# Part of V goes to the lower 64 partitions of two slots, in transfers of eight rows

## The chip, the cores and the metric

The kernel runs on one core of one Trainium2 chip. The metric is the device time of one execution in microseconds, as the median of several runs. A profile of one execution is read beside it: it lists each instruction of the engines (PE for matmuls, PEld for its weight loads, DVE, ACT, POOL, and SP, which issues the loads), and each packet of the 16 DMA engines.

## What is computed

Two layers of a decoder, each a cached attention with grouped heads and then a small network, for eight sequences and one new token each. Cut to the part that matters here, the attention:

```python
def _A_ref(x, k_cache, v_cache, wq, wo):          # x: (8, 1, 448)
    q = (x @ wq).reshape(B, 1, 16, 256).transpose(0, 2, 1, 3)
    k = jnp.repeat(k_cache, 2, axis=1)            # k_cache, v_cache: (8, 8, 4096, 256), bf16
    v = jnp.repeat(v_cache, 2, axis=1)
    scores = jnp.einsum("bhqd,bhkd->bhqk", q, k) * 256 ** -0.5
    p = softmax(scores)
    o = jnp.einsum("bhqk,bhkd->bhqd", p, v)
    return o.transpose(0, 2, 1, 3).reshape(B, 1, 4096) @ wo
x = x + _A_ref(_layernorm(x), k_cache, v_cache, wq, wo)
x = x + _B_ref(_layernorm(x), w1, w2, w3, w4)
...
```

Both layers use the same two caches. Each cache has 8 sequences x 8 heads x 4096 rows x 256 numbers of two bytes: 2 MB for each head of each sequence, 134 MB for a cache.

## The kernel before

**Tiles.** A head of K or V is read as 128 partitions of 32 consecutive rows each, 16 KB in a partition. It is cut into four pieces (`NCH`), each 4 KB of every partition: 512 KB. A piece lives in one of 31 slots of SBUF (`slots`, `NSLOT`). A load brings one, two or four neighbouring pieces at once into neighbouring slots (512 KB, 1 MB or 2 MB); `chunks` (lines 444 to 460) makes these groups, and its argument `most` is the largest. The planner may split a group when it finds no run of free slots.

**Pairs of heads.** Work goes by layer, sequence `b` and pair of heads `m`. `kpart` (line 836) takes the eight K pieces of a pair: most are transposed by DVE (line 914, into another slot), some by PE and ACT (lines 832 and 892), then PE makes the scores (lines 902, 923, 951) into the PSUM bank `psS`. Softmax follows (lines 983 to 1030); the probabilities are transposed into a small tile `pT`. `vpart` (line 1034) takes the eight V pieces of the pair. In the form used here PE multiplies each piece by its probabilities with four matmuls of 128 partitions x 512 columns (line 1089) into the bank `psV`. `pN` is a pair of small tiles that holds probabilities in another order for the pieces whose K was not transposed by DVE.

**Order.** The second layer of sequence b needs the first layer of the same sequence, so the body from line 1226 on goes through the sequences: `turn(b)` ends layer 0 of b and begins layer 1, then come the pairs of layer 1 of b and of layer 0 of b+1. `weave` lays the loads of K and V one between the other into one list, and SP issues all loads of the kernel in that order on one queue. `schedule` (line 168) is a planner that runs while the kernel is built: it simulates the engines with a cost for each operation, chooses a slot for each piece, and so fixes the order of instructions on every engine. In it an issue takes SP 330 ns (line 292), and a load starts 3.3 us after its issue at the earliest and moves at 410 or 415 bytes per ns (line 294).

**Waits.** A load waits on SP for the instructions that read its slot last. What uses a piece waits for the semaphore of its slot, which a load raises by 16 when it has landed, a sixteenth of that for each of the DMA engines that take part (line 1264).

Of the kernel before, what the change touches and what calls it, by code (L numbers as in the profile page):

```python
# [3 lines left out]
P = 128  # L4
B = 8
# [6 lines left out]
NCH = 4  # L12
NSLOT = 31
SMALL = 218
SLOT = 2048
# [5 lines left out]
NN = ((1, 0, 1, 1), (0, 0, 1, 1))  # L21
NZ = 2
WIDE = ((1, 0),)
MOST = (4, 4, 4, 2)
DRY4 = 4000.0
STILL = (False, False)
# [46 lines left out]
class Unit:  # L73


    def __init__(self, name, emit, nbytes, slotted=True):
        self.name, self.emit, self.nbytes, self.slotted = name, emit, nbytes, slotted
        self.wide = None
        self.slot = self.sem = self.val = None
        self.op = None  # L80
        self.readers = []
        self.land = None
        self.evs = [None, None]
        self.raw, self.source = False, None
        self.group, self.lead, self.pair = [self], None, None


class Plan:
# [79 lines left out]
    def schedule(self, order, nslot):  # L168
# [8 lines left out]
        free = {e: 0.0 for e in ("pe", "dve", "act", "pool", "sp")}  # L177
# [68 lines left out]
        while remaining or nxt[0] < len(order):  # L246
# [8 lines left out]
            while nxt[0] < len(order):  # L255
                u = order[nxt[0]]
                if any(d.end is None for d in u.op.deps):
                    break
                start = max(free["sp"], max((d.end + 80 for d in u.op.deps), default=0.0))
                us = u.group  # L260
                if u.slotted:
                    if len(us) == 1:
                        best = single(t)
                    else:
                        best, short = run(t, len(us))
                        if short and len(us) == 4 and transfer < t + DRY4:
                            order.insert(nxt[0] + 1, self.split(u, users))
                            us = u.group
                            best, short = run(t, len(us))
                        one = single(t)  # L270
                        if (len(us) == 2 and short and transfer < t + DRY and one is not None and slot_free[one][0] <= t + 1e-6
                                and len(slot_free) > bool(raw or u.raw) + sum(1 for o in ready["act"] if o.target is not None)
                                and free["sp"] <= t + 1e-6):
                            order.insert(nxt[0] + 1, self.split(u, users))
                            us, best = u.group, one
                    held = sum(1 for x in {o.target for o in ready["act"] if o.target is not None} if x.slot is None)
                    if best is None or len(slot_free) < len(us) + bool(raw or u.raw) + held:
                        break
                    start = max([start] + [slot_free[best + k][0] for k in range(len(us))])
                if start > t + 1e-6:  # L280
                    sp_next = start
                    break
                if u.slotted:
                    for k, x in enumerate(us):
                        _, waits = slot_free.pop(best + k)
                        x.slot = best + k
                        for w in waits:
                            u.op.deps[w] = True
                        live.append(x)
                        if x.raw:  # L290
                            raw.add(x)
                free["sp"] = start + 330.0
                if u.emit is not None:
                    transfer = max(start + 3300.0, transfer) + (P * 4096 * len(us) / 415.0 if len(us) > 1 else u.nbytes / 410.0)
                    land = transfer + 2000.0
                else:
                    land = start
                for x in us:
                    x.land = land
                u.op.on = "sp"  # L300
                seq["sp"].append(u.op)
                done(u.op, land, 0.0)
                nxt[0] += 1
                progress = True
            for e in ("pe", "dve", "act", "pool"):
# [15 lines left out]
                o = min(cand, key=lambda o: (o.prio, o.name))  # L321
# [37 lines left out]
def bass_interleave_layers__gqa_block_cached__mixer_s_mlp__decode_kernel(  # L359
# [26 lines left out]
    slots = [slab[:, SLOT * i:SLOT * i + SLOT] for i in range(NSLOT)]  # L386
# [6 lines left out]
    ident = sb("ident", [P, P], bf)  # L393
# [3 lines left out]
    pT = [sb(f"pT{i}", [P, 192], bf) for i in range(NP)]  # L397

    pN = [sb(f"pN{i}", [P, 48], bf) for i in range(NZ)]
# [17 lines left out]
    psS = [nc.alloc_psum_tensor(f"psS{i}", [P, 512], f32) for i in range(NS)]  # L417
    psV = [nc.alloc_psum_tensor(f"psV{i}", [P, 512], f32) for i in range(NV)]
# [7 lines left out]
    plan = Plan()  # L426
# [14 lines left out]
    U_wo = [rows(f"wo{i}", wo_sb[:, 8 * i:8 * i + 8, :], wo_src[:, 8 * i:8 * i + 8, :], P * 7168 * 1.1) for i in range(4)]  # L441
    U_w4 = [rows("w4", w4_sb[:, :, :], B_w4.rearrange("(t m) n -> m t n", m=P), P * 12544 * 1.1)]

    def chunks(cache, b, h, name, skip=(), most=2):


        src = cache[b, h].rearrange("(p j) d -> p (j d)", p=P)

        def emit(e, u):
            c, n = int(u.name[-1]), len(u.group)  # L450
            return e.dma_start(slab[:, SLOT * u.slot:SLOT * (u.slot + n)], src[:, SLOT * c:SLOT * (c + n)])
        us = [None if c in skip else Unit(f"{name}{c}", emit, P * 4096) for c in range(NCH)]
        for i in range(0, NCH, most):
            group = [u for u in us[i:i + most] if u is not None]
            if len(group) == most:
                plan.load(group[0], mates=group[1:])
            else:
                for u in group:
                    plan.load(u)
        return us  # L460


    Bc = Buf()
# [350 lines left out]
    def apart(t):  # L814

        return t.rearrange("p (a c u r) -> p a c r u", a=4, u=3, r=4)[:, :, :, :, 0:3:2]
# [19 lines left out]
    def kpart(at, layer, b, m, kept, most=2):  # L836
# [12 lines left out]
        nS[0] += 1  # L849
        p.x = x  # L850
        p.y = y = free_p.pop(0)
        p.z = z = free_n.pop(0) if layer == 0 and m > 1 else None
        plan.prio = at
        p.K, p.kload = [], []
        for s in range(2):
# [169 lines left out]
        for c in range(nn if z is None else 0):  # L1025
            ss = slice(sum(c >= w for w in nns), 2)
            add("act", lambda e, c=c, ss=ss: e.activation(apart(pT[y])[:, :, c, :, ss], xs.rearrange("p (a c r s) -> p a c r s", a=4, c=4, r=4)[:, :, c, :, ss],
                                                          ACT.Exp, scale=INV_SQRT_DH), 230, [], [BpT[y]], [bS[x]], prio=pr, name=n + f"pn{c}")
        add("pool", lambda g: g.partition_all_reduce(db, rs, P, ReduceOp.add), 450, [B_["pm"]], [B_["gm"]], prio=pr + 1, name=n + "db")
        R = add("dve", lambda e: e.reciprocal(rc, db), 70, [B_["gm"]], [Brc[y]], prio=pr + 1, name=n + "rc")  # L1030
        R.deps = {d: data or d.eng == "dve" for d, data in R.deps.items()}
# [2 lines left out]
    def vpart(at, p, still, bank, most, aside):  # L1034
# [2 lines left out]
        own_ = lambda s, c: z is not None and c < p.nns[s]  # L1037
        Bp = lambda s, c: [BpN[z]] if own_(s, c) else [BpT[y], BpZ[y]]
        plan.prio = at
        p.V = [u for s in range(2) for u in chunks(A_v_cache, b, 2 * m + s, f"{n}V{s}", (), most)]  # L1040
        p.vload = [u for u in p.V if u.lead is None]
        if layer == 0:
            out_, bo = o1[b % 2][:, 8 * m:8 * m + 8], Bo1[b % 2][m]
        else:
# [28 lines left out]
        else:  # L1073
# [3 lines left out]
            for s in range(2):  # L1077
                for c in range(NCH):
                    u = p.V[NCH * s + c]

                    def pv(e, u=u, c=c, s=s):
                        for i in range(4):
                            o = 12 * (NCH * i + p.place(s, c)) + 4 * s
                            w = pN[z][:, 12 * i + 4 * s:12 * i + 4 * s + 8] if own_(s, c) else pT[y][:, o:o + 8]
                            if c < p.nns[s]:
                                v = slots[u.slot][:, 512 * i:512 * i + 512].rearrange("p (k d) -> p k d", k=2)
                            else:
                                v = slots[u.slot].rearrange("p (k j d) -> p j k d", k=2, j=4)[:, i]
                            last = e.matmul(psV[x][32 * i:32 * i + 8, :].rearrange("p (k d) -> p k d", k=2), w, v,  # L1089
                                            start=(s == 0 and c == 0), stop=(s == 1 and c == NCH - 1))  # L1090
                        return last
                    o = add("pe", pv, 430, Bp(s, c), [], [bV[x]], [u], prio=at + 0.02 * (NCH * s + c), name=f"{n}V{s}{c}", n=4)
                    if s or c:
                        o.deps[first] = True
                    else:
                        first = o
# [24 lines left out]
                for d in Bq1[b].readers + Bq1[b].writers:  # L1121
                    O.deps.setdefault(d, False)
        free_p.append(y)
        if z is not None:
            free_n.append(z)

    Bst = [{k: Buf() for k in ("pm", "gm", "mx")} for _ in range(NS)]
    red, Bred = sf[:, 0:8], [Bs[k] for k in ("sq", "f", "f1")]
# [129 lines left out]
    for o in seq["sp"]:  # L1258
        u = o.unit
        if u.emit is None:  # L1260
            u.sem = None
            continue
        if u.slotted:
            slot_n[u.slot] += 16
            u.sem, u.val = slot_sem[u.slot], slot_n[u.slot]
        else:
            u.sem, u.val = nc.alloc_semaphore(f"s_{u.name}"), 16
# [124 lines left out]
```

## Time and profile before

| | |
|---|---|
| median of 3 runs | 1097.92 us (1097.88 to 1098.41) |
| the profiled execution | 1098.74 us |
| its span, first to last instruction | 1095.7 us |
| mean clock granted to TensorE | 0.619 of full speed |
| busy: DVE, PE, ACT, POOL | 832.6, 756.3, 207.8, 71.4 us |
| read from HBM | 446.77 MB, 408 GB/s over the span |
| loads of V: 2 MB, 1 MB, 512 KB | 50, 149, 14 |
| loads of K: 2 MB, 1 MB, 512 KB | 44, 71, 2 |

Times in the views count from the first instruction. A row of windows gives, for a stretch of time, the busy time of each engine with its number of instructions, the granted clock of TensorE, the share of time in which the 16 DMA engines were busy (it may pass 1 where packets of two queues overlap on one engine) and the rate in GB/s. A row of DMA issues gives the tile, the issuing queue, the count, the size of one and the median time from issue to landing. A row of waits says who waited for whom, how long in all, how often, and the longest.

### The profile page before, as it was taken

What the parts mean: (1) busy time and instruction counts of PE and PEld (TensorE: products, weight loads), DVE (VectorE), ACT (ScalarE), POOL (GpSimd) and SP (SyncE); (2) the same over time, 40 slices, a digit from 0 to 9 for tenths busy, and PEclk for the clock granted to TensorE, in tenths of its full rate; (3) what the DMA queues carried; (4) which work ended last, traced back from release to release, by engine and by line L of the source; (5) the groups of instructions that cost most, each with busy time, mean ns of one, the idle gap of its engine ahead of it and who ended that gap; (6) DMA issues with size and microseconds to landing.
All of it is one profiled execution on the core that took longest, in us unless ns stands there. A gap on an engine that the chain in (4) does not pass through costs nothing.

```text
span 1095.7 us, 33703 instructions
## 1 busy us (share of the span) xinstructions
PE 756.3 (69%) x15400; PEld 526.6 (48%) x15400; DVE 832.6 (76%) x1595; ACT 207.8 (19%) x314; POOL 71.4 (7%) x232
## 2 busy tenths in 40 slices
PE   2566586778577865867767787577666786676864
PEld 2355454465346543555436554355444654356533
DVE  4999459964997499955899469984799739995572
ACT  1032121112021211203112032121221121121210
POOL 0000000000000000000000000000100000000000
PEclk9997566556655665556655556555655566555665
DMA  9999999999999999999999999999999999999994
GB/s 353 406 419 420 395 406 426 422 412 408 429 423 415 412 425 427 421 405 409 424 426 420 411 412 429 426 417 394 427 427 423 419 399 428 427 422 411 410 427 176
DMA packets 54846, 448.94 MB, mean 410 GB/s; under 512 B 5536, under 2 KB 11568, under 8 KB 14128
## 3 DMA queue, kind: packets, MB, share of 16 engines
q1 hardware_dynamic: 54704, 446.80, 98.4%
q8 instruction: 120, 1.97, 0.7%
q14 instruction: 22, 0.18, 0.0%
HBM read 446.77 MB, written 0.01 MB: 408 GB/s over the span
## 4 chain that ended last, share of the span: by engine, by line
DVE 39%; DMA 24%; PE 21%; issue 9%; ACT 3%; POOL 0%; POOLq 0%; DVEq 0%
DVE slots L914 29%; DMA slots<-in_A_k_cache_dram 16%; DMA slots<-in_A_v_cache_dram 8%; PE psV L1089 6%; PE psS L923 5%; DVE pT L1021 2%; PE psT L678 2%; ACT slots L892 2%; PE psS L902 2%; DVE slots L1102 1%; PE psV L1063 1%; PE psT L607 1%; PE psK L832 1%; PE psT L1138 1%; DVE qe L643 1%
## 5 line engine op out<-in xcount | busy, mean ns | idle before, releaser
L914 DVE STREAM_TRANSPOSE slots<-slots 128x1024 bf16<-128x1024 bf16 x544 | 649.4, 1228 | 33.0 <-DMA slots<-in_A_k_cache_dram 24.3
L923 PE MATMUL psS<-qe,slots 128*128 128x8 bf16 x5760 | 225.3, 175 | 152.6 <-DVE slots L914 111.5
L923 PEld LDWEIGHTS psS<-qe,slots 128*128 128x128 bf16 x5760 | 191.1, 104 | 238.5 <-DVE slots L914 176.0
L1089 PE MATMUL psV<-slots,pT 128*8 128x512 bf16 x1528 | 181.1, 550 | 17.5 <-DMA slots<-in_A_v_cache_dram 9.5
L892 ACT COPY slots<-psK 128x1024 bf16<-128x1024 bf16 x80 | 78.8, 1014 | 168.0 <-PE psK L832 167.6
L832 PE MATMUL psK<-ident,slots 128*128 128x128 bf16 x640 | 74.2, 301 | 4.2 <-DMA slots<-in_A_k_cache_dram 4.1
L1100 ACT ACTIVATE slots<-psV 128x512 bf16<-128x512 f32 x48 | 29.0, 605 | 218.5 <-PE psV L1089 218.4
L985 POOL PARTITION_ALL_REDUCE small<-small x64 | 23.8, 372 | 693.5 <-DVE small L983 582.4
L832 PEld LDWEIGHTS psK<-ident,slots 128*128 128x128 bf16 x640 | 61.1, 138 | 7.0 <-DMA slots<-in_A_k_cache_dram 4.9
L1063 PE MATMUL psV<-pT,slots 128*128 128x2 bf16 x1568 | 50.9, 166 | 17.1 <-DMA slots<-in_A_v_cache_dram 15.9
L951 PE MATMUL psS<-slots,qe 128*8 128x512 bf16 x184 | 55.4, 587 | 6.7 <-DVE slots L914 5.4
L1063 PEld LDWEIGHTS psV<-pT,slots 128*128 128x128 bf16 x1568 | 47.3, 104 | 19.7 <-DMA slots<-in_A_v_cache_dram 16.1
L1089 PEld LDWEIGHTS psV<-slots,pT 128*8 128x8 bf16 x1528 | 31.5, 90 | 50.5 <-issue 20.9
L1021 DVE STREAM_TRANSPOSE pT<-psS 128x128 bf16<-128x128 bf16 x64 | 44.9, 702 | 6.5 <-PE psS L1013 4.7
L1006 ACT ACTIVATE pT<-psS 128x128 bf16<-128x128 f32 x56 | 15.5, 277 | 178.7 <-DVE psS L1003 178.6
L1066 DVE TENSOR_REDUCE small<-psV 128x8 f32<-128x32 f32 x16 | 2.8, 174 | 58.5 <-PE psV L1063 58.5
L1111 PE MATMUL psV<-same,slots 128*128 128x4 bf16 x320 | 14.0, 166 | 43.0 <-DVE slots L1102 36.9
L630 DVE TENSOR_TENSOR qe<-psT,small 128x32 bf16<-128x32 f32 x32 | 6.1, 190 | 48.2 <-PE psS L923 34.3
L902 PE MATMUL psS<-qo,slots 128*128 128x2 bf16 x768 | 27.8, 167 | 17.6 <-ACT slots L892 10.5
L1102 DVE TENSOR_TENSOR slots<-psV,slots 128x512 bf16<-128x512 f32 x48 | 32.3, 672 | 10.0 <-ACT slots L1100 10.0
L902 PEld LDWEIGHTS psS<-qo,slots 128*128 128x128 bf16 x768 | 24.0, 101 | 25.4 <-ACT slots L892 17.1
L1111 PEld LDWEIGHTS psV<-same,slots 128*128 128x128 bf16 x320 | 11.8, 102 | 49.2 <-issue 40.8
(170 smaller groups left out, 805.8 us busy)
## 6 DMA issues: line engine op xcount, KB each, us to landing
slots<-in_A_v_cache_dram SPq DMA_DIRECT2D x149, 1024.0 KB, 9.7
slots<-in_A_v_cache_dram SPq DMA_DIRECT2D x50, 2048.0 KB, 19.1
slots<-in_A_k_cache_dram SPq DMA_DIRECT2D x44, 2048.0 KB, 18.1
slots<-in_A_k_cache_dram SPq DMA_DIRECT2D x71, 1024.0 KB, 13.7
slots<-in_A_v_cache_dram SPq DMA_DIRECT2D x14, 512.0 KB, 8.1
wo_sb<-in_A_wo_dram SPq DMA_DIRECT2D x4, 896.0 KB, 19.5
wq_sb<-in_A_wq_dram SPq DMA_DIRECT2D x3, 1024.0 KB, 9.1
w_sb<-in_B_w_dram SPq DMA_DIRECT2D x1, 1568.0 KB, 16.9
```

Of the source, the lines that this page charges most:

```text
L832: last = e.transpose(tile[:, j * P:(j + 1) * P], slots[u.slot][:, o:o + P], ident[:, :])
L892: return e.copy(slots[u.slot][:, 1024 * t:1024 * t + 1024], tile)
L902: last = e.matmul(o, slots[u.slot][:, i:i + P], q, start=(cc == 0), stop=(cc == 1))
L914: return e.transpose(o, i)
L923: last = e.matmul(o, slots[u.slot][:, i:i + P], qe[:, 128 * k + 64 * s + 8 * g:128 * k + 64 * s + 8 * g + 8], start=(g == 0), stop=(g == 7))
L951: last = e.matmul(o, q, K[:, lo:hi + 1:hi - lo, :, g, :], start=(g == 0), stop=(g == 7))
L1021: add("dve", lambda e: e.transpose(pZ[:, :, 0:3:2].rearrange("p n s r -> p n r s"), psS[x][:, 128:192].bitcast(bf).rearrange("p (n r s) -> ...
L1063: last = e.matmul(o, slots[u.slot][:, i:i + P], w, start=(j == 0), stop=(j == 7))
L1089: last = e.matmul(psV[x][32 * i:32 * i + 8, :].rearrange("p (k d) -> p k d", k=2), w, v, start=(s == 0 and c == 0), stop=(s == 1 and c == ...
L1100: add("act", lambda e: e.activation(part(0), psV[x][:, :], ACT.Copy), 590, [], [Bhalf[0]], [bV[x]], [v], prio=at - 1, name=n + "ve0").targ ...
L1102: add("dve", lambda e: e.tensor_tensor(part(1), psV[x][:, :], part(0), ALU.subtract), 590, [Bhalf[0]], [Bhalf[1]], [bV[x]], [v], prio=at - ...
L1111: last = e.matmul(to[:, 4 * cc:4 * cc + 4].rearrange("p (s h) -> p s h", s=2), part(k // 2)[:, i:i + P], w, start=(k == 0), stop=(k == 3))
```

## The change

`LOW(layer, b, m, s)` picks one head in eight places: the first head of pair 0, for layer 0 of sequence 0 and for layer 1 of sequences 0 to 6. Of this head's V the last of the four pieces (`LOWC` = 3) is loaded in another way. Before, its 512 KB went, as part of a larger load, to 128 partitions of one slot. Now the rows of partitions 0 to 63 go to the lower 64 partitions of one slot, and the rows of partitions 64 to 127 to the lower 64 partitions of a second slot. Each half is moved by eight transfers of eight rows of 4 KB, the rows of one transfer being eight partitions apart; all eight raise the slot's semaphore, by 128 together. The head's other pieces are loaded as 1 MB and 512 KB. The two halves are separate units in the list of loads, so a load of K stands between them.

PE multiplies such a piece with eight matmuls of 64 partitions instead of four of 128: for the second half the probabilities of partitions 64 to 127 are needed on partitions 0 to 63. One matmul with the identity moves them into free columns of `psS`, and ACT copies them into a tile of `pN`. The product waits for both halves and for this tile. In the planner an issue of such a half costs eight times 330 ns, and its 256 KB are priced at 410 bytes per ns. The diff, without its empty lines:

```diff
@@ -21,6 +21,10 @@
 NN = ((1, 0, 1, 1), (0, 0, 1, 1))
 NZ = 2
 WIDE = ((1, 0),)
+LOWS, LOWC = 0, 3
+def LOW(layer, b, m, s):
+    return s == LOWS and m == 0 and (layer == 1 and b < B - 1 or layer == 0 and b == 0)
 MOST = (4, 4, 4, 2)
 DRY4 = 4000.0
 STILL = (False, False)
@@ -83,6 +87,8 @@
         self.evs = [None, None]
         self.raw, self.source = False, None
         self.group, self.lead, self.pair = [self], None, None
+        self.upper = None
+        self.issues = 1
 class Plan:
@@ -289,7 +295,7 @@
                         live.append(x)
                         if x.raw:
                             raw.add(x)
-                free["sp"] = start + 330.0
+                free["sp"] = start + 330.0 * u.issues
                 if u.emit is not None:
                     transfer = max(start + 3300.0, transfer) + (P * 4096 * len(us) / 415.0 if len(us) > 1 else u.nbytes / 410.0)
                     land = transfer + 2000.0
@@ -441,7 +447,9 @@
     U_wo = [rows(f"wo{i}", wo_sb[:, 8 * i:8 * i + 8, :], wo_src[:, 8 * i:8 * i + 8, :], P * 7168 * 1.1) for i in range(4)]
     U_w4 = [rows("w4", w4_sb[:, :, :], B_w4.rearrange("(t m) n -> m t n", m=P), P * 12544 * 1.1)]
-    def chunks(cache, b, h, name, skip=(), most=2):
+    def chunks(cache, b, h, name, skip=(), most=2, low=False):
         src = cache[b, h].rearrange("(p j) d -> p (j d)", p=P)
@@ -450,13 +458,28 @@
             c, n = int(u.name[-1]), len(u.group)
             return e.dma_start(slab[:, SLOT * u.slot:SLOT * (u.slot + n)], src[:, SLOT * c:SLOT * (c + n)])
         us = [None if c in skip else Unit(f"{name}{c}", emit, P * 4096) for c in range(NCH)]
+        if low:
+            def half(p0):
+                def emit(e, u):
+                    for i in range(8):
+                        d = e.dma_start(slots[u.slot][i:64:8, :], src[p0 + i:p0 + 64:8, SLOT * LOWC:SLOT * (LOWC + 1)])
+                        if i < 7:
+                            d.then_inc(u.sem, 16)
+                    return d
+                return emit
+            most = 2
+            us[LOWC] = Unit(f"{name}{LOWC}", half(0), 64 * 4096)
+            us[LOWC].upper = Unit(f"{name}u{LOWC}", half(64), 64 * 4096)
+            us[LOWC].issues = us[LOWC].upper.issues = 8
         for i in range(0, NCH, most):
             group = [u for u in us[i:i + most] if u is not None]
-            if len(group) == most:
+            if len(group) == most and all(u.upper is None for u in group):
                 plan.load(group[0], mates=group[1:])
             else:
                 for u in group:
-                    plan.load(u)
+                    for w in (u, u.upper):
+                        if w is not None:
+                            plan.load(w)
         return us
@@ -849,7 +872,9 @@
         nS[0] += 1
         p.x = x
         p.y = y = free_p.pop(0)
+        p.low = LOW(layer, b, m, LOWS)
         p.z = z = free_n.pop(0) if layer == 0 and m > 1 else None
+        p.zl = zl = free_n.pop(0) if p.low else None
         plan.prio = at
         p.K, p.kload = [], []
         for s in range(2):
@@ -1026,6 +1051,12 @@
             ss = slice(sum(c >= w for w in nns), 2)
             add("act", lambda e, c=c, ss=ss: e.activation(apart(pT[y])[:, :, c, :, ss], xs.rearrange("p (a c r s) -> p a c r s", a=4, c=4, r=4)[:, :, c, :, ss],
                                                           ACT.Exp, scale=INV_SQRT_DH), 230, [], [BpT[y]], [bS[x]], prio=pr, name=n + f"pn{c}")
+        if p.low:
+            low = psS[x][0:64, 192:208].rearrange("p (a r) -> p a r", a=4)
+            add("pe", lambda e: e.matmul(low, ident[:, 64:P], apart(pT[y])[:, :, p.place(LOWS, LOWC), :, LOWS], start=True, stop=True),
+                110, [BpT[y], Bc], [], [bS[x]], prio=pr, name=n + "lo", n=1)
+            add("act", lambda e: e.copy(apart(pN[zl])[0:64, :, 0, :, LOWS], low), 230, [], [BpN[zl]], [bS[x]], prio=pr, name=n + "lc")
         add("pool", lambda g: g.partition_all_reduce(db, rs, P, ReduceOp.add), 450, [B_["pm"]], [B_["gm"]], prio=pr + 1, name=n + "db")
         R = add("dve", lambda e: e.reciprocal(rc, db), 70, [B_["gm"]], [Brc[y]], prio=pr + 1, name=n + "rc")
         R.deps = {d: data or d.eng == "dve" for d, data in R.deps.items()}
@@ -1037,8 +1068,8 @@
         own_ = lambda s, c: z is not None and c < p.nns[s]
         Bp = lambda s, c: [BpN[z]] if own_(s, c) else [BpT[y], BpZ[y]]
         plan.prio = at
-        p.V = [u for s in range(2) for u in chunks(A_v_cache, b, 2 * m + s, f"{n}V{s}", (), most)]
-        p.vload = [u for u in p.V if u.lead is None]
+        p.V = [u for s in range(2) for u in chunks(A_v_cache, b, 2 * m + s, f"{n}V{s}", (), most, LOW(layer, b, m, s))]
+        p.vload = [w for u in p.V if u.lead is None for w in (u, u.upper) if w is not None]
         if layer == 0:
             out_, bo = o1[b % 2][:, 8 * m:8 * m + 8], Bo1[b % 2][m]
         else:
@@ -1078,6 +1109,14 @@
                 for c in range(NCH):
                     u = p.V[NCH * s + c]
+                    def low(e, u=u, c=c, s=s):
+                        for i in range(4):
+                            o, i_ = 12 * (NCH * i + p.place(s, c)) + 4 * s, 12 * i + 4 * s
+                            for w, v in ((pT[y][0:64, o:o + 8], u), (pN[p.zl][0:64, i_:i_ + 8], u.upper)):
+                                last = e.matmul(psV[x][32 * i:32 * i + 8, :].rearrange("p (k d) -> p k d", k=2), w,
+                                                slots[v.slot][0:64].rearrange("p (k j d) -> p j k d", k=2, j=4)[:, i], start=False, stop=False)
+                        return last
                     def pv(e, u=u, c=c, s=s):
                         for i in range(4):
                             o = 12 * (NCH * i + p.place(s, c)) + 4 * s
@@ -1089,7 +1128,10 @@
                             last = e.matmul(psV[x][32 * i:32 * i + 8, :].rearrange("p (k d) -> p k d", k=2), w, v,
                                             start=(s == 0 and c == 0), stop=(s == 1 and c == NCH - 1))
                         return last
-                    o = add("pe", pv, 430, Bp(s, c), [], [bV[x]], [u], prio=at + 0.02 * (NCH * s + c), name=f"{n}V{s}{c}", n=4)
+                    if u.upper is not None:
+                        o = add("pe", low, 860, Bp(s, c) + [BpN[p.zl]], [], [bV[x]], [u, u.upper], prio=at + 0.02 * (NCH * s + c), name=f"{n}V{s}{c}", n=8)
+                    else:
+                        o = add("pe", pv, 430, Bp(s, c), [], [bV[x]], [u], prio=at + 0.02 * (NCH * s + c), name=f"{n}V{s}{c}", n=4)
                     if s or c:
                         o.deps[first] = True
                     else:
@@ -1121,8 +1163,9 @@
                 for d in Bq1[b].readers + Bq1[b].writers:
                     O.deps.setdefault(d, False)
         free_p.append(y)
-        if z is not None:
-            free_n.append(z)
+        for z_ in (z, p.zl):
+            if z_ is not None:
+                free_n.append(z_)
     Bst = [{k: Buf() for k in ("pm", "gm", "mx")} for _ in range(NS)]
     red, Bred = sf[:, 0:8], [Bs[k] for k in ("sq", "f", "f1")]
@@ -1261,7 +1304,7 @@
             u.sem = None
             continue
         if u.slotted:
-            slot_n[u.slot] += 16
+            slot_n[u.slot] += 16 * u.issues
             u.sem, u.val = slot_sem[u.slot], slot_n[u.slot]
         else:
             u.sem, u.val = nc.alloc_semaphore(f"s_{u.name}"), 16
```

## The prediction

> **What bounds the kernel now.** First the page's rows of DMA, then the queues:
>
> ```profile
> span 1095.7 us, 33703 instructions
> ...
> DMA  9999999999999999999999999999999999999994
> ...
> q1 hardware_dynamic: 54704, 446.80, 98.4%
> q8 instruction: 120, 1.97, 0.7%
> q14 instruction: 22, 0.18, 0.0%
> ```
>
> The 16 DMA engines are busy in every slice but the last; no compute engine is (DVE 76%, PE 69%). So the loads set the time, and the question is which engine of the sixteen. For that I read the trace's DMA packets and semaphore increments one by one. Within one engine a packet starts where the last one ended, so each engine's chain can be followed. Per engine a 1 MB load (eight packets of 8 KB) takes 2.485 us, a 2 MB load 4.89, a 512 KB load (eight of 4 KB) 1.265, that is 0.158 a packet. Over all loads (94 of 2 MB, 223 of 1 MB, 16 of 512 KB, and 21.2 us of wo, w3, w4 and the wqt halves) this makes 1055.3 us for each engine.
>
> The 120 packets of q8 are PE's instructions, 16 KB each. A packet of q8 lengthens the chain of one engine by 1.54 us, and fetch n and fetch n+8 hit the same one: eight engines take them all in turn. 120 x 1.54 / 8 = 23.1 us for each of these eight (call them the fetch half). The 8 KB packets of q14 (about 1 us each, some 20 of them) fell on the other eight: 2.5 us each (the free half). So the fetch half needs 1055.3 + 23.1 = 1078.4 us. Loads run from 2.2 us to the last landing at 1082.2, which is 1080: the fetch half is never idle and sets the time. The free half, 1057.8, has some 20 us to spare. It shows: the 16 increments of one load are 1.5 to 2 us apart at a batch's start and 4 to 4.6 at its end, then the free half runs dry because no slot comes free, as here:
>
> ```profile
> core 0: us, PE busy (x) PEld busy (x) DVE busy (x) ACT busy (x) POOL busy (x), PEclk, DMA share, GB/s
> 8.00:13.00 5.00, 0.26 (x4) 0.18 (x4) 1.56 (x17) 0.00 (x0) 0.28 (x1) 1.00 1.02 424
> 12.90:15.40 2.50, 1.99 (x20) 1.73 (x20) 1.38 (x11) 1.02 (x2) 0.00 (x0) 1.00 1.09 243
> ...
> 499.50:501.50 2.00, 2.00 (x32) 0.68 (x24) 1.54 (x7) 1.10 (x2) 0.00 (x0) 0.71 0.88 266
> ```
>
> In the last row the engines' share falls to 0.88 and the rate to 266 GB/s. The middle row is the other thing to see: there the two wqt loads go to 64 partitions each. All engines are busy (1.09), yet they move 243 GB/s where a load of 128 partitions moved 424 just before. Packets that go to one half of the partitions hold each other up; in the records these eight 4 KB packets took 2.86 us of each engine, 0.357 each, against 0.158.
>
> **Which half gets the new packets.** An 8-row transfer starts eight chains at once (the A_x load: eight packets within 0.06 us). After an idle time the free half's engines start 0.95 to 1.21 us after the issue (22 of the 25 such starts that I could find), while the sixteen of the first K load start from 0.98 to over 1.45 us: the free half is served first. I take it that an 8-row transfer uses these. [...]
>
> **The change part by part.** *Loads.* After the change the SP order has 80 loads of 2 MB, 243 of 1 MB, 24 of 512 KB and 128 of 8 rows (the piece's group is split, and so are some K loads, as a slot more is held). For all engines: 80 x 4.89 + 243 x 2.485 + 24 x 1.265 + 21.2 = 1046.6 us, 8.7 less. The fetch half then needs 1046.6 + 23.1 = 1069.7. The free half has 128 packets of 4 KB more, 16 for each of eight pieces, each with its own semaphore packet (9 ns and a gap: 0.013): 1046.6 + 2.5 + 128 t.
>
> *The price t* is not in the trace. From below: the pace of a 512 KB load, 0.158 + 0.013 = 0.171, so 1071.0. From above: the pace of wqt, 0.357, so 1094.8. The rows of one transfer are eight partitions apart, in one half of the partitions, so it is nearest to wqt, where packets of the same size go to one half. The windows of 1 us from 13 to 16 us move 193, 254 and 238 GB/s, 1.86 times less than 424. I take 1.86 x 0.158 + 0.013 = 0.307: 128 x 0.307 = 39.3, and the free half needs 1088.4. That is 10.0 more than the 1078.4 that set the time before. The point where it turns is t = (1078.4 - 1049.1) / 128 = 0.229.
>
> Against wqt as a measure stands that there sixteen engines met in one half and here only eight: eight at full pace, half of 424, is 212 GB/s, less than the 243 that half took. Only if the eight meet on fewer targets do they slow down. [...]
>
> *Issues.* 128 transfers take the place of eight parts of loads. Issues that follow each other are 0.43 to 0.47 us apart (45.44 to 45.91 in SP's timeline), so 8 x 0.47 = 3.8 us for each group of eight, 60 us in all, and all later loads queue behind them on SP. What hides it is what is already queued:
>
> ```profile
> slots<-in_A_v_cache_dram SPq DMA_DIRECT2D x50, 2048.0 KB, 19.1
> slots<-in_A_k_cache_dram SPq DMA_DIRECT2D x44, 2048.0 KB, 18.1
> ...
> SPq L451 <- PE psV L1089: 284.6, 83, 11.8
> SPq L451 <- PE psS L923: 255.8, 79, 11.2
> ```
>
> The pieces stand among the 2 MB loads, which land 18 to 19 us after their issue, and SP spends most of its time waiting for PE to free a slot. So 0 on the path; without that cover up to 3.8 us a group.
>
> *PE and ACT.* A piece takes eight matmuls for four (4 x 0.59 us by L1089's median), one matmul with ident (0.29, L1013) and one ACT copy (0.31, L1027): under 3 us for each of eight pieces, hidden by the 31% in which PE is idle. PE's matmuls of the piece now wait for two landings, the second after a 2 MB K load; the planner prices a half at 0.64 us (64 x 4096 / 410) while the free half needs 8 x 0.307 = 2.5. PE may so stand up to 3.7 us at a piece, with later scores and V products behind it and SP behind their slots; the queued 11 to 25 us cover that too. POOL and DVE get nothing.
>
> Sum: +10.0 us. Against the profiled execution, 1095.7 of span and 1098.74 in all, that is 1108.7; against the median of 1097.92 it is 1107.9, which I round to **1108**.
>
> **Rivals.**
> *The eight engines keep their pace* (chance 0.30, faster). The place is the free half, the price 0.171 a packet, and it decides wherever t stays under 0.229. Then the fetch half's 1069.7 and the free half's 1071.0 nearly meet, and the time falls by 7.4: 1090.5. For it: eight engines need 212 GB/s and one half of the partitions took 243; the shift is about half of the 20 us by which the halves differ. Against it: the pattern by eighths, and 0.357 in wqt.
> *The fetches fall on the half that gets the packets* (0.12, slower). That half then needs 1046.6 + 23.1 + 128 t: 1091.6 at t = 0.171 and 1109.0 at 0.307, so 13 to 31 us more, 1111 to 1129. For it: three of the 25 starts after an idle time came late (over 1.21 us). Against it: the other 22.
> *It evens out* (0.10, no change): t near 0.229, or the 8-row transfers fall on all sixteen engines in turn, so that nothing is shifted and the 8.7 us come back as their packets. The eight chains of A_x speak against the latter. 1098.
>
> **How the numbers follow.** The forecast, t over 0.25, has 0.48. Slower by over 0.2% (2.2 us, about what a measurement of this kernel can tell from no change): 0.48 + 0.12 = 0.60; within: 0.10; faster: 0.30. The likeliest case's own range is t from 0.25 to 0.357: 1049.1 + 32.0 or 45.7 against 1078.4, +2.7 to +16.4, 1101 to 1114. The whole range starts at 1090, which holds the faster case but its best end (the fetch half alone, -8.7), and ends at 1115, which leaves out the upper part of the same-half case.
>
> **What would show it.** Right: the 8-row packets of 4 KB take about 0.3 us, and in the deep part of each batch it is now the other eight engines that land last; the 16 landings of a load are then apart by as much as before, in the other order. The DMA share stays at 1.0 and the rate in windows around the pieces falls under 400 GB/s. Wrong on t: packets of 0.16 to 0.18 and landings of a load under 3 us apart at a batch's end. Wrong on the half: landings over 6 us apart. Wrong on the cover: DMA shares under 0.95 around the pieces while SP issues, or longer PE waits for V loads than the 9.5 us of L1089 on the page. The forecast fails altogether if the span changes with all of this unchanged.

## The result, and the profile after

| | before | after |
|---|---|---|
| median | 1097.91 us (1097.88 to 1098.41) | 1146.27 us (1139.81 to 1147.37) |
| span of the profiled execution | 1095.7 us | 1144.6 us |
| ratio of the times | | 1.0427 (95% interval 1.0388 to 1.0466) |

The changed kernel is slower by 48 us; 10 were forecast. First the rows of DMA on its page, then the queues:

```profile
span 1144.6 us, 33899 instructions
...
DMA  9999999999999999999999999999999999999994
GB/s 347 335 422 419 395 417 375 417 402 386 380 411 406 400 387 403 423 378 407 361 427 420 391 407 358 427 408 372 421 369 425 405 375 405 390 423 406 378 428 182
...
q1 hardware_dynamic: 58768, 446.80, 97.9%
q8 instruction: 121, 1.98, 0.7%
q14 instruction: 24, 0.19, 0.1%
```
The DMA engines are still busy in every slice but the last, and the bytes are the same 446.80 MB. But the rate has deeper dips than before: about one slice in each sequence falls to 335 to 380 GB/s. Before, only the first and the last slice were under 394:

```profile
GB/s 353 406 419 420 395 406 426 422 412 408 429 423 415 412 425 427 421 405 409 424 426 420 411 412 429 426 417 394 427 427 423 419 399 428 427 422 411 410 427 176
```
So the engines have not become idle; they have become slower at certain times. Whatever needs data waits longer for it, as the groups and the DMA issues of the page show (in a group, behind the second bar: idle time ahead of it and what ended most of that; the first two groups are those of the kernel before):

```profile
L914 DVE STREAM_TRANSPOSE slots<-slots 128x1024 bf16<-128x1024 bf16 x544 | 649.4, 1228 | 33.0 <-DMA slots<-in_A_k_cache_dram 24.3
L1089 PE MATMUL psV<-slots,pT 128*8 128x512 bf16 x1528 | 181.1, 550 | 17.5 <-DMA slots<-in_A_v_cache_dram 9.5
...
L939 DVE STREAM_TRANSPOSE slots<-slots 128x1024 bf16<-128x1024 bf16 x544 | 648.6, 1227 | 60.7 <-DMA slots<-in_A_k_cache_dram 57.4
...
L1128 PE MATMUL psV<-slots,pT 128*8 128x512 bf16 x1496 | 186.8, 564 | 26.0 <-DMA slots<-in_A_v_cache_dram 17.2
...
slots<-in_A_v_cache_dram SPq DMA_DIRECT2D x41, 2048.0 KB, 20.8
...
slots<-in_A_k_cache_dram SPq DMA_DIRECT2D x39, 2048.0 KB, 22.8
...
slots<-in_A_v_cache_dram SPq DMA_DIRECT2D x128, 32.0 KB
```
DVE's transposes wait 57.4 us for loads of K (24.3 before), and the V products of layer 1 17.2 us for V (9.5 before). The 2 MB loads of V and K land 20.8 and 22.8 us after their issue, for 19.1 and 18.1. The slots come free later, and SP waits for them as before (waits of SP: total, times, longest):

```profile
SPq L459 <- PE psS L948: 277.8, 81, 17.2
SPq L459 <- PE psV L1128: 245.5, 69, 7.9
```
The dips lie at the pieces. Here is the piece of sequence 2, whose transfers SP issues from 408.8 to 419.0 us, and whose packets land from 420.5 to 426.3 and from 428.8 to 434.7 us (rows of windows, the last two columns are the DMA share and GB/s; a packet counts whole in the window in which it starts, so the share of a short window can pass 1):

```profile
core 0: us, PE busy (x) PEld busy (x) DVE busy (x) ACT busy (x) POOL busy (x), PEclk, DMA share, GB/s
...
418.00:420.00 2.00, 0.00 (x0) 0.00 (x0) 2.00 (x3) 0.07 (x1) 0.00 (x0) 0.93 1.07 428
420.00:422.00 2.00, 0.88 (x15) 0.91 (x16) 2.00 (x3) 0.00 (x0) 0.00 (x0) 0.50 1.11 258
422.00:424.00 2.00, 2.00 (x18) 1.15 (x17) 2.00 (x5) 1.01 (x1) 0.00 (x0) 0.50 1.09 303
424.00:426.00 2.00, 2.00 (x20) 1.07 (x17) 2.00 (x3) 0.00 (x0) 0.00 (x0) 0.50 0.89 287
426.00:428.00 2.00, 1.17 (x25) 1.00 (x22) 2.00 (x5) 1.01 (x1) 0.19 (x1) 0.86 1.02 428
428.00:430.00 2.00, 1.58 (x57) 1.45 (x53) 2.00 (x4) 0.69 (x1) 0.18 (x1) 0.99 1.12 275
430.00:432.00 2.00, 0.68 (x16) 0.42 (x13) 1.38 (x6) 0.27 (x1) 0.52 (x2) 0.50 0.94 311
432.00:434.00 2.00, 1.55 (x14) 1.33 (x15) 1.57 (x2) 0.48 (x1) 0.00 (x0) 0.50 1.03 305
```
While the first half lands, the rate falls from 428 to 258, 303 and 287 GB/s; between the halves it is 428 again; while the second half lands, it is 275 to 311. The share stays near 1. Over these six windows the rate is 138 GB/s under the 428 on average: 12 us x 138 / 428 = 3.9 us lost at this one piece.

The records of single packets say who lost them. Of the packets that start between 187 and 188 us, in another piece, the 20 of 4 KB took 0.225 us on average, the 11 of 8 KB 0.470 and the 9 of 16 KB 0.887 (none under 0.786). Usual are 0.159, 0.309 and 0.611. On average they are 1.4 to 1.5 times as long, and the 8 KB and 16 KB packets are those of ordinary loads. They run on all sixteen engines, not only on the eight that move the piece. An engine's packets can be followed from one to the next, as in most cases the next starts 3 or 4 ns before the last one ends. At the piece of sequence 2, while its first half moves, the eight chains without any packet of the piece have their 16 KB packets lengthened 1.46 to 1.55 times. Summed over the run, the packets take 1120.7 us for each engine where those of the kernel before took 1077.8.

### The profile page after: what moved, and what is told of

Its sections match the earlier page's. It is cut to its first block, busy times and chain, and to the rows that moved or that the text cites. A ratio compares the mean times of both kernels' runs of the same rounds, so it can differ in the third digit from the quotient of the medians.

```text
span 1144.6 us, 33899 instructions
## 1 busy us (share of the span) xinstructions
PE 770.1 (67%) x15416; PEld 525.9 (46%) x15416; DVE 834.2 (73%) x1595; ACT 209.0 (18%) x322; POOL 71.5 (6%) x232
## 3 DMA queue, kind: packets, MB, share of 16 engines
q1 hardware_dynamic: 58768, 446.80, 97.9%
## 4 chain that ended last, share of the span: by engine, by line
DMA 49%; DVE 20%; PE 17%; issue 6%; SPq 5%; ACT 2%; POOL 0%; POOLq 0%; DVEq 0%
DMA slots<-in_A_k_cache_dram 27%; DMA slots<-in_A_v_cache_dram 21%; DVE slots L939 13%; PE psV L1128 5%; PE psS L948 3%; SPq L465 2%; SPq L438 2%; PE psT L701 2%; PE psV L1094 1%; PE psT L630 1%; ACT slots L917 1%; PE psS L927 1%; DVE pT L1046 1%; DVE slots L1144 1%; PE psT L1181 1%
## 5 line engine op out<-in xcount | busy, mean ns | idle before, releaser
L939 DVE STREAM_TRANSPOSE slots<-slots 128x1024 bf16<-128x1024 bf16 x544 | 648.6, 1227 | 60.7 <-DMA slots<-in_A_k_cache_dram 57.4
L1128 PE MATMUL psV<-slots,pT 128*8 128x512 bf16 x1496 | 186.8, 564 | 26.0 <-DMA slots<-in_A_v_cache_dram 17.2
L976 PE MATMUL psS<-slots,qe 128*8 128x512 bf16 x208 | 52.6, 602 | 5.6 <-DVE slots L939 5.6
L1181 PE MATMUL psT<-small,wo_sb 128*128 128x1 bf16 x1024 | 33.2, 166 | 2.9 <-DVE small L1157 1.8
## 6 DMA issues: line engine op xcount, KB each, us to landing
slots<-in_A_v_cache_dram SPq DMA_DIRECT2D x41, 2048.0 KB, 20.8
slots<-in_A_k_cache_dram SPq DMA_DIRECT2D x39, 2048.0 KB, 22.8
```

The costliest lines, as they stand in the source:

```text
L939: return e.transpose(o, i)
L976: last = e.matmul(o, q, K[:, lo:hi + 1:hi - lo, :, g, :], start=(g == 0), stop=(g == 7))
L1181: last = e.matmul(psT[:, 4 * (2 * s + i) + c:4 * (2 * s + i) + c + 1], wo_sb[:, a, d0:d0 + P], o1[b % 2][:, a:a + 1], start=(k == 0), stop ...
```

## The experiments

Four theories stood against each other: TARGETS (the packets to every eighth partition meet on few targets and hold up everyone), ISSUES (SP's many issues let the engines run dry), ORDER (two slots, split groups, PE waiting for two landings), and HALF or SHIFT (the eight engines that get the packets are not the ones with time to spare). Time of the kernel before beside all runs: 1097.8 to 1098.2 us.

| run | time, us | ratio to before, 95% interval |
|---|---|---|
| changed kernel, rows eight apart | 1146.3 | 1.0388 to 1.0466 |
| rows four apart (four) | 1111.9 | 1.0103 to 1.0143 |
| 16 rows four apart (sixteen) | 1123.1 | 1.0192 to 1.0245 |
| 64 rows at once (whole) | 1135.6 | 1.0311 to 1.0354 |
| ordinary transfers of 2 KB (flat) | 1100.0 | 1.0009 to 1.0027 |
| flat with small extra transfers (tiny) | 1114.6 | 1.0127 to 1.0161 |
| four without the first piece (four7) | 1107.7 | 1.0068 to 1.0098 |
| four, to the upper partitions (upper4) | 1152.3 | 1.0467 to 1.0513 |
| four apart and eight apart (half8) | 1127.6 | 1.0240 to 1.0289 |
| changed kernel without the first piece (after7) | 1141.2 | 1.0363 to 1.0417 |

**Rows four apart.** One index is changed:

```diff
-                        d = e.dma_start(slots[u.slot][i:64:8, :], src[p0 + i:p0 + 64:8, SLOT * LOWC:SLOT * (LOWC + 1)])
+                        r = 32 * (i // 4) + i % 4
+                        d = e.dma_start(slots[u.slot][r:r + 29:4, :], src[p0 + r:p0 + r + 29:4, SLOT * LOWC:SLOT * (LOWC + 1)])
```

> The changed kernel, with the rows of each 8-row transfer four partitions apart (all within 32 partitions) instead of eight apart; number of transfers, slots, PE and ACT work and the whole order stay. Four theories for the 48 us (1097.9 to 1146.3). TARGETS: packets to every eighth partition meet on few targets and hold up the packets of all sixteen engines; then the loss goes with the spacing: 16 KB packets around a piece stay near 0.61 us (0.86 to 1.2 in the changed kernel) and the time falls to 1090 to 1111 (1090 if the shifted packets lie on the half without instruction fetches, 1111 if on the half with them: 1046.6 + 23.1 + 128 x 0.171 against 1078.4). ISSUES: 16 issues of 0.606 us, 9.7 us of SP for a piece, let the engines run dry; unchanged here, so 1140 or more. ORDER: two slots, split groups, PE waiting for two landings; unchanged, 1140 or more. HALF alone (the packets fall on the half that has the fetches, at 0.31 each): between, some 1111. [...]

Measured 1111.9: 34.4 us of the 48.4 are gone with the spacing alone. The windows of the same piece, whose halves land here from 410.8 to 414.1 and from 417.0 to 421.6 us:

```profile
core 0: us, PE busy (x) PEld busy (x) DVE busy (x) ACT busy (x) POOL busy (x), PEclk, DMA share, GB/s
...
410.00:412.00 2.00, 0.83 (x15) 0.86 (x16) 2.00 (x3) 0.00 (x0) 0.00 (x0) 0.69 1.03 416
412.00:414.00 2.00, 2.00 (x18) 1.15 (x18) 2.00 (x5) 1.01 (x1) 0.00 (x0) 0.50 1.13 473
414.00:416.00 2.00, 1.77 (x26) 1.21 (x22) 2.00 (x3) 0.19 (x1) 0.00 (x0) 0.96 1.00 426
416.00:418.00 2.00, 0.31 (x12) 0.31 (x13) 2.00 (x5) 0.82 (x1) 0.14 (x1) 1.00 0.98 406
418.00:420.00 2.00, 1.58 (x58) 1.49 (x55) 2.00 (x4) 0.69 (x1) 0.23 (x1) 1.00 1.03 430
420.00:422.00 2.00, 1.40 (x29) 1.06 (x26) 1.75 (x7) 1.02 (x2) 0.52 (x2) 0.75 1.02 434
```
No dip is left; in the changed kernel the windows of this piece showed 258 to 311. At each of the later seven pieces, in the 30 us from its first issue, 2 to 4 of the 395 to 646 packets of 16 KB take over 1.2 times their usual time; with rows eight apart it is 113 to 168. The 4 KB packets are at 0.161. The time alone would fit HALF too, which gave some 1111; but HALF had the new packets at 0.31 each and nothing changed beside them, and the packets say otherwise. So the spacing makes the 34 us, as TARGETS has it, though no run shows a target or counts them. What remains, 14 us, is not explained by that.

**16 rows, and 64 rows.** In sixteen, each half goes in four transfers of 16 rows four apart, in whole in one of 64 rows:

```diff
# sixteen
-                    for i in range(8):
+                    for i in range(4):
...
+                        d = e.dma_start(slots[u.slot][i:64:4, :], src[p0 + i:p0 + 64:4, SLOT * LOWC:SLOT * (LOWC + 1)])
# whole
+                    return e.dma_start(slots[u.slot][0:64, :], src[p0:p0 + 64, SLOT * LOWC:SLOT * (LOWC + 1)])
```

> As the run before, but each half goes in four transfers of 16 rows four apart, so that all sixteen engines take part and no packet is shifted to eight engines. TARGETS with the packets on the free half: the shift was worth something, so this one is 5 to 9 us slower than rows four apart in eights (about 1098 to 1101: 1046.6 + 16 x 4 x 0.171 + 23.1 = 1080.6 against 1078.4, +2.2). HALF: this one is faster than eights by up to 11 us (128 x 0.171 / 2). ISSUES: 8 issues for a piece instead of 16, so about half of the 48 us, some 1122. ORDER: 1140 or more.

> The changed kernel with each half in one transfer of 64 rows to partitions 0 to 63 (four 4 KB packets on each of sixteen engines), one issue for eight; the rest and the planned order stay. TARGETS: here the 64 rows go to all targets of the lower half; by the wqt row, 0.357 a packet, 16 x 4 x 0.357 = 22.8 for every engine, 1046.6 + 22.8 + 23.1 = 1092.5, +14, about 1112; at 0.171 it is +2, 1100. ISSUES: the issues are gone, so back to 1098 to 1105. ORDER: 1140 or more. HALF: nothing is shifted, 1100 to 1112.

1123.1 and 1135.6: both far slower than TARGETS gave (1098 to 1101, and 1100 to 1112), and both with fewer issues than four. The 1123.1 lies beside the 1122 that ISSUES gave, but whole, with one issue for eight, should then have come back to 1098 to 1105. So ISSUES can't be the main cause, and TARGETS as I had it is incomplete: in sixteen the rows are four apart as in four, and yet 65 to 122 of the 16 KB packets around a piece are slow again, for 2 to 4. What differs is that a transfer has 16 rows, over 64 partitions, instead of 8 within 32.

**The control.** The two slots, the split groups, all of PE's and ACT's work and the planned order stay; only the way of loading is an ordinary one:

```diff
+                    f = SLOT * LOWC + SLOT // 2 * (p0 // 64)
+                    return e.dma_start(slots[u.slot][:, 0:SLOT // 2], src[:, f:f + SLOT // 2])
```

> The control: the changed kernel's two slots, split groups, eight matmuls, identity matmul, ACT copy and planned order, but each half of the piece is loaded as 2 KB of all 128 partitions in one ordinary transfer, and PE reads that (the piece's products are then of other values than the reference's). ORDER: 1140 or more. All three others: only the plain bytes are left, 16 x about 0.65 = 10 us for every engine, 1046.6 + 10.4 + 23.1 = 1080 against 1078.4, so 1097 to 1103.

1100.0: ORDER is worth 2.2 us and no more.

**Issues or shift?** Between flat and four lie 11.9 us.

```diff
+                    for i in range(7):
+                        e.dma_start(slots[u.slot][i % 4:i % 4 + 29:4, SLOT // 2 + 32 * i:SLOT // 2 + 32 * i + 32], src[i % 4:i % 4 + 29:4, f:f + 32]).then_inc(u.sem, 16)
                     return e.dma_start(slots[u.slot][:, 0:SLOT // 2], src[:, f:f + SLOT // 2])
```

> The control (flat, 1100.0) with seven more 8-row transfers of 64 bytes a row ahead of each half, into a part of the slot that nobody reads: SP issues as often as in the changed kernel (16 for a piece), with next to no bytes (7 x 16 packets of about 0.05 us on eight engines, at most 5.6 us for one of them). If SHIFT (the packets on eight engines, some of which are those with the instruction fetches) makes the 11.9 us between flat (1100.0) and rows four apart (1111.9): 1100 to 1104. If the ISSUES of SP make them: 1112.

1114.6, which by the expectation would speak for ISSUES. It does not decide: the small packets are not cheap. Each takes 0.011 us, but at the piece of sequence 2 the next 16 KB packet of eight engines behind each half's seven takes 1.21 to 1.51 us instead of 0.61. That puts some 0.6 to 0.9 us on these eight engines sixteen times, about as much as the 4 KB packets of four do. As a test of the issues this run failed.

```diff
-    return s == LOWS and m == 0 and (layer == 1 and b < B - 1 or layer == 0 and b == 0)
+    return s == LOWS and m == 0 and (layer == 1 and b < B - 1)
```

> Rows four apart (1111.9) without the piece of layer 0 in sequence 0, so seven pieces for eight. The delay of rows four apart against the kernel before is 3.6 us by the third pair of heads and grows to 14 to 16 over the rest. SHIFT: every piece costs 16 x 0.171 - 1.27 = 1.5 on the engines that set the time, so 1 to 2 us less, 1110. START: the first piece costs 3.6 because nothing is queued yet behind which SP's issues could hide: 1108.

1107.7: the first piece alone costs 4.2 us. Why, the windows at its second half show, first of flat, then of the changed kernel:

```profile
core 0: us, PE busy (x) PEld busy (x) DVE busy (x) ACT busy (x) POOL busy (x), PEclk, DMA share, GB/s
...
45.00:50.00 5.00, 2.14 (x46) 1.44 (x43) 5.00 (x7) 0.00 (x0) 0.00 (x0) 1.00 1.04 422
50.00:55.00 5.00, 3.21 (x49) 1.21 (x45) 4.26 (x4) 0.00 (x0) 0.00 (x0) 1.00 1.02 424
```
```profile
core 0: us, PE busy (x) PEld busy (x) DVE busy (x) ACT busy (x) POOL busy (x), PEclk, DMA share, GB/s
...
45.00:50.00 5.00, 2.14 (x43) 1.35 (x40) 5.00 (x7) 0.00 (x0) 0.00 (x0) 1.00 0.63 210
50.00:55.00 5.00, 2.63 (x44) 1.03 (x40) 2.16 (x2) 0.00 (x0) 0.00 (x0) 1.00 0.96 351
```
In the changed kernel SP is held up by the loads of wo until 42.4 us, then spends 6.6 us on eight transfers of 32 KB, and nothing else is queued: the share falls to 0.63 and the rate to 210 GB/s. In four it is 0.66. So ISSUES is right for this piece, and only there as far as the shares show: at the later ones the share of four stays at 0.95 or above while SP issues.

**Own partitions.** Two assumptions are left for the pace of four: the eight rows need different targets (DISTINCT), or each engine needs the partitions that it writes in ordinary loads (OWN). Rows four apart from partition 0 can't tell these apart; rows four apart from partition 64 can:

```diff
-                        d = e.dma_start(slots[u.slot][r:r + 29:4, :], src
+                        d = e.dma_start(slots[u.slot][64 + r:64 + r + 29:4, :], src
```

> Rows four apart, but to partitions 64 to 127 of the two slots instead of 0 to 63 (PE multiplies them with the probabilities of partitions 64 to 127 in both halves, so the products of the piece are of other values). DISTINCT: eight rows that reach eight different targets keep their pace wherever they are, 1112. OWN: in the ordinary loads each engine writes always the same few partitions, the eight engines of an 8-row transfer those of the lower half; above they meet the other eight engines in their places, so packets slow down again (16 KB above 0.75 us around the pieces): 1120 to 1146. [...]

1152.3, the slowest of all, with the same spacing as four. The piece of sequence 2, first half landing from 423.2 to 430.8 us, second from 432.0 to 439.9:

```profile
core 0: us, PE busy (x) PEld busy (x) DVE busy (x) ACT busy (x) POOL busy (x), PEclk, DMA share, GB/s
...
424.00:426.00 2.00, 2.00 (x17) 1.26 (x15) 2.00 (x3) 0.71 (x1) 0.00 (x0) 0.51 1.15 252
426.00:428.00 2.00, 1.30 (x21) 0.84 (x17) 2.00 (x3) 0.66 (x1) 0.00 (x0) 1.00 0.97 293
428.00:430.00 2.00, 1.26 (x48) 1.27 (x48) 2.00 (x7) 0.35 (x1) 0.37 (x1) 0.84 0.98 313
430.00:432.00 2.00, 1.40 (x34) 1.02 (x31) 1.72 (x6) 0.95 (x2) 0.10 (x1) 0.50 1.01 363
432.00:434.00 2.00, 0.00 (x0) 0.00 (x0) 0.75 (x3) 0.00 (x0) 0.43 (x2) 0.50 1.02 223
434.00:436.00 2.00, 0.00 (x0) 0.00 (x0) 0.00 (x0) 0.00 (x0) 0.00 (x0) 0.50 0.96 285
```
The rates are as low as in the changed kernel, and stay low for longer. DISTINCT, which gave 1112, is wrong. OWN, which gave 1120 to 1146, comes nearer and has the direction right; it stays my assumption, as no run numbers the engines or shows which partitions one of them writes. What the runs show is that the spacing does not decide alone: the same rows four apart took 1111.9 us in the lower 64 partitions and 1152.3 in the upper.

**The dose.** In half8 the first half of a piece goes with rows four apart and the second with rows eight apart; after7 is the changed kernel without its first piece (the same edit as in four7).

```diff
+                        r, k, w = (32 * (i // 4) + i % 4, 4, 29) if p0 == 0 else (i, 8, 57)
+                        d = e.dma_start(slots[u.slot][r:r + w:k, :], src[p0 + r:p0 + r + w:k, SLOT * LOWC:SLOT * (LOWC + 1)])
```

> Half the dose of the spacing: of each piece the first half goes with rows four apart, the second with rows eight apart. Rows four apart gave 1111.9, rows eight apart 1146.3. If the loss belongs to each packet that is out of its place (OWN), it is linear in them: 1111.9 + 34.4 / 2 = 1129, and about 65 of the 16 KB packets around a piece over 1.2 times their usual time, for 116 to 167. If it comes from the two halves meeting each other or from a backlog that builds up over a piece: under 1120.

> The changed kernel (rows eight apart) without the piece of layer 0 in sequence 0. Rows four apart gained 4.2 us by leaving it out (1111.9 to 1107.7), of which 1.5 are its share of SHIFT and the rest the START, where the DMA share is 0.66 while SP issues with nothing queued. With rows eight apart the packets' own loss of this piece comes on top, if it is the same as for the other pieces: 34.4 / 8 = 4.3, so 1146.3 - 4.2 - 4.3 = 1138. If at the start, with little else in flight, spacing costs nothing: 1142.

1127.6 with 64 to 86 slow packets of 16 KB around a piece: about half the loss for half the packets. After7 gives 1141.2, nearer to the 1142 of little in flight, but its runs lie from 1138.5 to 1144.2, so they do not rule out 1138. The packets of the first piece say both: its first half is slow as elsewhere (4 KB packets of 0.240 us on average, and a rate of 295 and 301 GB/s from 32 to 36 us), while in its second half, which SP brings one by one, they average 0.199 and 30 of the 64 take at most 0.164, about the usual 0.159. The other seven pieces cost about 1141.2 - 1107.7 = 33.5 by the spacing, 4.8 each.

## Why the prediction was wrong

In the differences of the runs, each uncertain by some us where rows are eight apart, the 48.4 us are: 2.2 for slots, splits, PE, ACT and order (flat against before); 4.2 for the first piece (four against four7); 7.6 for the packets on eight engines at the other seven pieces (1107.7 - 1097.9 - 2.2); and 34.4 for the spacing (changed kernel against four). Step by step:

- *The engines with the instruction fetches set the time* (1055.3 + 23.1). This held. The same sum for flat, 1046.6 + 23.1 + 16 x 0.67 = 1080.4 (0.67 for eight packets of 2 KB at 0.085, less their overlap, and a semaphore packet), stands against 1082.2 from the first load to the last landing. For four7, which has 85 loads of 2 MB, 234 of 1 MB, 23 of 512 KB and 112 packets of 0.174, it is 1047.4 + 23.1 + 19.5 = 1090.0 against 1089.7.
- *The price t of a packet* was taken as 0.307, with bounds of 0.171 and 0.357. Around a piece the 4 KB packets of the changed kernel average 0.207 to 0.230, those of an ordinary load among them, so t is about 0.24. With rows four apart it is 0.174. The size was a quarter too high. So was the upper bound of 0.357 from wqt: its 128 packets take 0.288 us on average.
- *The ordinary packets were charged at their old pace*, in "for all engines: 80 x 4.89 + 243 x 2.485 + ...". **This is the step that failed.** The packets of the other loads, on all sixteen engines, became slower too. Against four, 16 KB packets took 20.0 us more for each engine, 8 KB packets 5.0, and 4 KB packets, those of the piece among them, 7.8: together 32.8 of the 34.4 us. I charged the collision to the packets that the change adds and nothing to those beside them. The trace before would have said so, at wqt: from 14.5 to 16 us, the 27 packets of 8 KB of the loads behind it, which run beside and just behind its last 4 KB packets, took 0.54 to 0.60 us in the mean of each half microsecond, for 0.31 usually.
- *Packets to rows eight apart meet on fewer targets.* This was my assumption; no run shows a target. The direction was right for the rows of the changed kernel and of four: 4 KB packets took 0.207 to 0.230 us around a piece with rows eight apart and 0.161 with rows four apart. The spacing is not the whole reason: upper4 has that of four and took 1152.3 us.
- *The eight engines are the free half.* Wrong. That the free half starts first after an idle time (22 of 25 starts) did not say which engines an 8-row transfer uses. With t = 0.174 the sum gave about 1091 on this assumption; four measured 1111.9, and without first piece and order's part still about 1105. The landings of one load in four, in us after its first, show how the packets fell (ahead of the piece of sequence 2, and behind it):

```
ahead   0.00 0.10 0.40 0.67 0.68 0.81 0.98 1.13 1.60 1.84 1.87 1.94 2.07 2.11 2.25 3.07
behind  0.00 0.25 1.41 1.43 1.66 1.69 1.82 2.13 2.20 2.63 2.77 2.97 3.10 4.79 5.05 5.28
```

  The piece puts 16 x 0.174 = 2.8 us on eight of them. On the eight early ones alone, the spread would not have grown; on the eight late ones alone, eight would now stand over 4. There are three over 4 and two under 1, so the packets fell on some of either kind, and an engine with both sets the end. For the time this is the second rival (fetches on the half that gets the packets), to which I had given 0.12: its sum for t = 0.171 was 1091.6 for such an engine, and four's loads took 1094.5 from the first to the last landing, some 1.7 of it idle at the first piece. At all seven later pieces of four the spread grows, by 1.3 to 2.5 us. The chains of packets show the mixture directly: in four the fetches at 417.3 and 427.3 us stand in chains that carry all sixteen packets of the piece of sequence 2, those at 536.6 and 552.8 us in chains that carry none of the next piece. No run here names an engine, and how many of the eight take fetches was not counted.
- *SP's issues are hidden.* Held for seven pieces: in four the packets of a half start there 10.3 to 15.1 us after its first issue, and SP needs some 5 us for the eight. Not for the first, for which I had named the price (3.8 us a group without cover) but not looked whether the cover was there. The issues are 0.606 us apart, not 0.47.
- *PE and ACT are hidden.* Held: 2.2 us with all the rest of the order.

Of the signs that I had named, the rate under 400 GB/s around the pieces, the landings over 6 us apart (6.9 for the load behind the second piece; "wrong on the half") and the longer wait of PE for V (17.2 for 9.5) all came. The last of them I had put to the cover, and most of it does belong there: PE waits 6.0 us for V in flat, 14.2 in four and 6.2 in four7, so the first piece makes 8 us of it, and the pace the rest.

## What to carry to other kernels

A transfer to few partitions is to be priced together with what is in flight beside it: here 4 MB in an unusual layout slowed 113 to 168 neighbouring packets of 16 KB at each of the later seven pieces, and the packets of 16 KB took 20.0 us more for each engine than in four, those of 4 KB, with the piece's own, 7.8. If small transfers must run beside large loads, measure more than one layout of their rows and count the slow packets beside them: here eight rows four apart left 2 to 4 slow packets of 16 KB at a piece in the lower 64 partitions (1111.9 us), sixteen rows four apart 65 to 122 (1123.1 us), and the eight rows four apart took 1152.3 us in the upper 64 partitions. Neither the number of issues nor the spacing alone gave that order. Before the spare time of some DMA engines is used, find out which ones the transfer will really run on, by following the packets of a trace or by the landings of the loads behind it.

## What the hardware showed that was not expected

- In the collision, all engines were slowed about alike: 4, 8 and 16 KB packets ran at 18.2, 17.4 and 18.5 bytes per ns (from 0.225, 0.470 and 0.887 us), for 26 to 27 usually, though at the piece of sequence 2, while its first half moved, eight of the sixteen chains carried no packet of it (their 16 KB packets took 1.46 to 1.55 times as long). Why those are drawn in was not settled.
- Seven transfers of eight rows of 64 bytes hardly take any time of an engine (7 x 0.011 us and their semaphore packets), and yet its next 16 KB packet takes 0.6 to 0.9 us longer. Behind the 4 KB packets of four it was not so: there 2 to 4 of the 395 to 646 packets of 16 KB around a piece took over 1.2 times their usual 0.611 us.
- Loads to 64 partitions were slow beyond wqt, whose 4 KB packets took 0.288 us on average for 0.159 usually: one ordinary-looking transfer of 64 rows for each half cost 35.6 us over eight pieces (1135.6 of whole against 1100.0 of flat).
